# A planned spectral and gated-linear kernel: the fifth column class put together on GpSimd, with one table and one matmul per frequency

## The chip, the cores and the metric

The kernel runs on one core of one Trainium2 chip. Its time is the device time of one execution in microseconds (us); smaller is better. The engines are TensorE (PE in the profile, its weight loads PEld), VectorE (DVE), ScalarE (ACT), GpSimd (POOL) and SyncE (SP), which issues nearly all DMAs.

## What is computed

```python
xn = layernorm(x)                          # x: (1, 2048, 640) bf16
X  = rfft2(xn) * (w_r + 1j * w_i)          # 2048 x 321 complex weights
A  = irfft2(X, s=(2048, 640))
B  = ((xn @ w_gate) * (xn @ w_up)) @ w_down    # 640 -> 1536 -> 640, no nonlinearity
out = x + bf16(A) + B
```

Two branches share the normalized input: a global spectral filter over rows and columns, and a bilinear gated unit.

## The kernel before

**Stages.** The 2048 rows are held as 16 row blocks of 128 (block b, line 356 on). Each block is normalized: statistics by VectorE (`bn_stats`, L756, `bn_aggr`, L765) for blocks 0 to 5 or by ScalarE (two passes with an accumulator, L738 and L747) for the others, a square root on ScalarE (L775), a reciprocal (L782), and the scaling. For blocks 0 to 3 the scaling is two VectorE instructions, `sub` (L792, subtract the mean, which needs no root) and `mul` (L798); for the others it is one (L799). Blocks 0 to 3 are transposed by PE (`T0`, L818), the others by a DMA transpose (L806).

The gated branch is `GU` (PE, L948 for four blocks at a time, L968 for the first blocks), its evictions `eG` (ScalarE L684 or VectorE L685), the product `H` (L984, L985), and at the end the accumulations `ACC` (L1224), which share their PSUM bank with the last step of the spectral branch, `IV` (L1236), and go out through `FINA`, `FIN` and the output DMAs.

The spectral branch splits the 640 columns by residues (`S1` to `S5`, VectorE, L860 to L895) and the rows by a 64-point transform (`R`, PE, L908). Then 16 steps t of two frequencies each follow, which is the stage that the change is about: `D` (PE, L1025) transforms along columns, `eD` evicts, `C` (PE, L1045) finishes the rows, `WM` (VectorE, L1062 for four column classes, L1068 for the fifth) multiplies with the filter weights, and `IA` (PE, L1116 and L1118) starts the way back for each of the 32 frequencies q; `eIA` evicts it. After all 32 comes `I` (PE, L1147), `eI`, the recombination `V1` to `V5` on VectorE, and `IV`.

**The two ways of complex multiplication.** The 321 spectral columns fall into five classes. For classes one to four, `WM` writes the products with w_r and w_i of two steps t (a pair), `SM` (L1089, L1090) adds and subtracts halves of the partitions into the tile `L`, and `JA`, `JB` (L1101 and a copy on L684 or L685) fill the mirrored half of `L`. `IA` then needs one matmul per class, with the table `ti[:, q, 0]`. For the fifth class there is no addition: `WM` writes its two products into `Y5` (three buffers, `_NY`), `NS` on GpSimd (L1077 to L1079, three instructions for each t) makes mirrored and negated copies, and PE does the complex addition by accumulating two matmuls (L1118) with the tables `ti[:, q, 0]` and `ti[:, q, 1]`:

```python
for k in range(4):
    c.e.matmul(ps[:, bk, 64 * k:64 * k + 64], yl[:, k:512:4], v_ti[:, q, 0, :], start=True, stop=True)
for i in range(2):
    ins = c.e.matmul(ps[:, bk, 256:320], v_y5[:, yr, g, 128 * i:128 * i + 128], v_ti[:, q, i, :],
                     start=(i == 0), stop=(i == 1))
```

**What sets the order.** Every task above is created by `T(...)` in a fixed sequence, with the engines that it may run on and a duration that was assumed for it. The list `_PLAN` gives, for each task by its number in that sequence, the engine (0 PE, 1 ScalarE, 2 VectorE, 3 GpSimd, 4 SP) and the PSUM bank. `replay` (L151) follows the list; the engines run their tasks strictly in that order. `compute_waits` (L196) turns dependencies into semaphore waits; buffers that share memory depend on each other. The name of any place in the list is found by counting the tasks in order of creation.

**The head.** PE first runs 40 warm-up matmuls (L720) on a tile that VectorE sets to zero (L696), then `T0_0`, ten small matmuls (`fill`, L709), and the first `GU` groups, as their weights land. Of the down-projection weights, blocks 7 to 11 are loaded early; blocks 0 to 6 share memory with the table `ti` and are loaded when the last `IA` has read it.

Of the kernel before, what the change touches and what calls it, by code (L numbers as in the profile page):

```python
# [71 lines left out]
class _Sched(object):  # L72
# [123 lines left out]
    def compute_waits(self):  # L196
        allt = sorted(self.tasks, key=lambda t: (t.start, t.tid))
# [58 lines left out]
def _build_tables():  # L256
# [65 lines left out]
    ti = np.zeros((128, _NQ, 2, 64), np.float64)  # L322
    for q in range(_NQ):
        k = _rows(q, npm, nk1)
        ph = two_pi * ((s1[:, None] * k[None, :]) % _S) / _S
        c = np.exp(-1j * ph)
        pm = np.broadcast_to(npm[None, :], (64, 64))
        f = np.where(ck == 1, np.where(pm == 1, -1j, 1j), 1.0 + 0j)
        if q == 0:
            f = (ck == pm).astype(np.complex128)  # L330
        fm = c * f
        im = (np.conj(c) * f / _S).T
        tf[0:64, q, n_re] = fm.real
        tf[0:64, q, n_im] = fm.imag
        tf[64:128, q, n_re] = -fm.imag
        tf[64:128, q, n_im] = fm.real
        ti[n_re, q, 0] = im.real
        ti[n_im, q, 0] = -im.imag
        ti[n_re, q, 1] = im.imag
        ti[n_im, q, 1] = im.real  # L340
# [21 lines left out]
_WD_LOADS = ((7, 12), (0, 2), (2, 4), (4, 6), (6, 7))  # L362
_FT_ORDER = (7, 8, 9, 10, 11, 0, 1, 2, 3, 4, 5, 6)
# [6 lines left out]
_NY = 3  # L370
# [29 lines left out]
def _d_act(n):  # L400
# [4 lines left out]
    (12, 4, -1), (0, 1, -1), (13, 4, -1), (176, 1, -1), (175, 4, -1), (8, 2, -1), (19, 2, -1), (9, 3, -1), (177, 4, -1),  # L405
    (18, 2, -1), (20, 2, -1), (11, 0, 0), (23, 2, -1), (21, 1, -1), (22, 2, -1), (24, 2, -1), (29, 2, -1), (25, 0, 2),
    (28, 2, -1), (26, 1, -1), (27, 2, -1), (178, 4, -1), (10, 0, 4), (14, 4, -1), (30, 2, -1), (33, 2, -1), (31, 1, -1),
    (32, 2, -1), (187, 0, 5), (34, 2, -1), (185, 0, 4), (188, 1, -1), (35, 0, 6), (15, 4, -1), (37, 2, -1), (192, 0, 5),
    (190, 0, 0), (186, 1, -1), (189, 2, -1), (38, 2, -1), (179, 4, -1), (36, 1, -1), (39, 2, -1), (180, 4, -1), (181, 4, -1),
    (197, 0, 1), (40, 2, -1), (48, 2, -1), (41, 1, -1), (43, 2, -1), (42, 2, -1), (193, 1, -1), (195, 0, 2), (44, 2, -1),  # L410
    (47, 2, -1), (202, 0, 3), (200, 0, 4), (182, 4, -1), (191, 1, -1), (196, 1, -1), (198, 1, -1), (49, 2, -1), (50, 1, -1),
    (16, 4, -1), (194, 2, -1), (201, 1, -1), (45, 0, 2), (52, 2, -1), (51, 2, -1), (183, 4, -1), (53, 2, -1), (207, 0, 6),
    (46, 1, -1), (184, 4, -1), (199, 2, -1), (118, 2, -1), (54, 0, 7), (205, 0, 2), (1, 4, -1), (203, 1, -1), (204, 2, -1),
    (55, 1, -1), (210, 0, 3), (212, 0, 7), (217, 0, 5), (208, 1, -1), (17, 4, -1), (215, 0, 4), (119, 2, -1), (206, 1, -1),
    (209, 2, -1), (120, 2, -1), (56, 2, -1), (211, 1, -1), (60, 2, -1), (59, 2, -1), (2, 4, -1), (3, 4, -1), (57, 2, -1),
    (68, 1, -1), (69, 1, -1), (213, 1, -1), (220, 0, 0), (121, 2, -1), (4, 4, -1), (58, 2, -1), (70, 1, -1), (216, 1, -1),
    (61, 2, -1), (218, 1, -1), (62, 1, -1), (122, 2, -1), (63, 2, -1), (222, 0, 1), (5, 4, -1), (214, 2, -1), (64, 2, -1),
    (125, 0, 2), (221, 1, -1), (71, 1, -1), (223, 1, -1), (123, 0, 6), (126, 1, -1), (219, 2, -1), (227, 0, 4), (127, 2, -1),
    (232, 0, 5), (225, 0, 0), (72, 1, -1), (230, 0, 1), (224, 2, -1), (128, 2, -1), (6, 4, -1), (7, 4, -1), (228, 1, -1),
    (66, 2, -1), (78, 1, -1), (79, 1, -1), (237, 0, 4), (226, 1, -1), (129, 2, -1), (235, 0, 0), (73, 2, -1), (80, 1, -1),  # L420
    (233, 1, -1), (229, 2, -1), (81, 1, -1), (130, 2, -1), (231, 1, -1), (82, 1, -1), (240, 0, 5), (76, 2, -1), (131, 2, -1),
    (238, 1, -1), (134, 0, 2), (74, 2, -1), (236, 1, -1), (83, 2, -1), (234, 2, -1), (242, 0, 4), (84, 2, -1), (65, 4, -1),
    (245, 0, 1), (67, 4, -1), (241, 1, -1), (75, 4, -1), (88, 1, -1), (77, 4, -1), (239, 2, -1), (135, 1, -1), (252, 0, 0),
    (247, 0, 5), (136, 2, -1), (243, 1, -1), (89, 1, -1), (244, 2, -1), (246, 1, -1), (132, 0, 2), (137, 2, -1), (90, 1, -1),
    (91, 1, -1), (86, 2, -1), (248, 1, -1), (250, 0, 1), (249, 2, -1), (255, 0, 4), (92, 1, -1), (98, 1, -1), (251, 1, -1),
    (85, 4, -1), (87, 4, -1), (437, 4, -1), (438, 4, -1), (93, 2, -1), (99, 1, -1), (138, 2, -1), (439, 4, -1), (253, 1, -1),
    (257, 0, 5), (256, 1, -1), (100, 1, -1), (258, 1, -1), (96, 2, -1), (254, 2, -1), (101, 1, -1), (139, 2, -1), (260, 0, 1),
    (262, 0, 0), (267, 0, 4), (94, 2, -1), (263, 1, -1), (133, 1, -1), (102, 1, -1), (261, 1, -1), (259, 2, -1), (140, 2, -1),
    (265, 0, 5), (103, 2, -1), (266, 1, -1), (440, 4, -1), (268, 1, -1), (270, 0, 0), (143, 0, 2), (264, 2, -1), (441, 4, -1),
    (104, 2, -1), (272, 0, 1), (124, 1, -1), (141, 0, 4), (269, 2, -1), (442, 4, -1), (108, 1, -1), (271, 1, -1), (273, 1, -1),  # L430
    (277, 0, 6), (149, 2, -1), (274, 2, -1), (109, 1, -1), (275, 0, 7), (280, 0, 0), (443, 4, -1), (142, 1, -1), (282, 0, 1),
    (444, 4, -1), (276, 1, -1), (278, 1, -1), (147, 0, 4), (281, 1, -1), (445, 4, -1), (145, 0, 6), (150, 2, -1), (446, 4, -1),
    (285, 0, 0), (106, 2, -1), (110, 1, -1), (283, 1, -1), (447, 4, -1), (146, 1, -1), (111, 1, -1), (287, 0, 1), (279, 2, -1),
    (112, 1, -1), (144, 1, -1), (292, 0, 6), (151, 2, -1), (286, 1, -1), (290, 0, 7), (293, 1, -1), (113, 2, -1), (448, 4, -1),
    (284, 2, -1), (152, 2, -1), (288, 1, -1), (116, 2, -1), (291, 1, -1), (297, 0, 2), (474, 4, -1), (475, 4, -1), (289, 2, -1),
    (476, 4, -1), (295, 0, 3), (114, 2, -1), (153, 2, -1), (302, 0, 0), (294, 2, -1), (162, 2, -1), (298, 1, -1), (296, 1, -1),
    (95, 4, -1), (97, 4, -1), (105, 4, -1), (299, 2, -1), (303, 1, -1), (154, 0, 6), (148, 1, -1), (107, 4, -1), (300, 0, 1),
    (477, 4, -1), (301, 1, -1), (156, 0, 2), (158, 0, 4), (159, 1, -1), (305, 0, 0), (155, 1, -1), (478, 4, -1), (160, 0, 4),
    (310, 0, 1), (479, 4, -1), (163, 2, -1), (480, 4, -1), (481, 4, -1), (307, 0, 6), (308, 1, -1), (304, 2, -1), (115, 4, -1),
    (312, 0, 7), (306, 1, -1), (164, 2, -1), (315, 0, 6), (317, 0, 0), (309, 2, -1), (313, 1, -1), (157, 1, -1), (311, 1, -1),  # L440
# [82 lines left out]
def _build(nc, A_x, A_w_r, A_w_i, B_w_gate, B_w_up, B_w_down, out, opts=None):  # L523
# [3 lines left out]
    with es:  # L527
# [167 lines left out]
        def em_wz(c):  # L695
            return c.e.memset(v_dum, 0.0)  # L696
# [651 lines left out]
```

## Time and profile before

| What | Value |
|---|---|
| Median of 8 runs | 199.52 us (199.22 to 200.2) |
| The profiled execution | 199.36 us |
| Its span in the profile | 197.0 us |
| PE busy | 190.5 us, 97% of the span |
| VectorE busy | 177.6 us, 90% |
| ScalarE busy | 137.9 us, 70% |
| GpSimd busy | 28.4 us, 14%, 53 instructions |
| DMA | 23.78 MB, mean 121 GB/s |

The profile covers the span from the first to the last instruction of the program; the profiled execution's time is 2.36 us longer. Busy time of PE counts matmuls whose ends are modelled, so that a matmul row's mean is longer than the distance from one matmul to the next; the distance is read from the starts in the timeline. A few matmul records are missing (404 of the 420 on L948 are there).

### The profile page before, as it was taken

The numbers are of one execution on the slowest core, as the hardware profiler recorded it, in microseconds if no ns is written. First come the engines' busy times: TensorE is split into PE (matmuls) and PEld (weight loads), VectorE is DVE, ScalarE is ACT, GpSimd is POOL, SyncE is SP. The second block draws the span as 40 slices with busy tenths as digits, with TensorE's granted clock in tenths as the row PEclk, the third lists the DMA queues.
The fourth block names the chain that finished last, engine by engine and source line by source line (L and its number), as shares of the span: only waits on it lengthen the run. The fifth ranks groups of instructions, "written<-read, shape, count | busy, mean of one in ns | idle before, by whom it ended". The sixth has DMA issues, their size and how long they took to land.

```text
span 197.0 us, 4284 instructions
## 1 busy us (share of the span) xinstructions
PE 190.5 (97%) x1607; PEld 122.4 (62%) x1623; DVE 177.6 (90%) x396; ACT 137.9 (70%) x299; POOL 28.4 (14%) x53
## 2 busy tenths in 40 slices
PE   7799999999999999999999999999999999999995
PEld 7698645444554555555555555557777777777774
DVE  3799999999999989999899998995999999989743
ACT  3378999999965789999999999966414342334220
POOL 0000000000000003545163460760000000000000
PEclk9999999999999999999999999999999999999999
DMA  6999995245549232542452402003400434233422
GB/s 178 305 328 372 388 137 100 47 120 120 129 88 296 86 85 54 133 101 56 117 148 55 120 17 67 2 3 104 128 3 0 136 100 124 76 103 119 147 70 67
DMA packets 29667, 23.78 MB, mean 121 GB/s; under 512 B 10576, under 2 KB 27600, under 8 KB 29520
## 3 DMA queue, kind: packets, MB, share of 16 engines
q1 hardware_dynamic: 28848, 23.16, 42.6%
q10 hardware_dynamic: 800, 0.36, 0.6%
q8 instruction: 13, 0.21, 0.5%
q14 instruction: 6, 0.05, 0.1%
HBM read 18.92 MB, written 2.62 MB: 109 GB/s over the span
## 4 chain that ended last, share of the span: by engine, by line
PE 88%; DVE 6%; ACT 1%; issue 1%; DMA 1%
PE ps L948 41%; PE ps L1224 26%; PE ps L968 7%; PE ps L1147 2%; PE ps L1236 2%; PE ps L908 2%; PE ps L1116 2%; PE ps L1025 2%; PE ps L1045 2%; DVE arena L685 1%; ACT arena L684 1%; DVE arena L1062 1%; DMA arena<-in_A_x_dram 1%; PE ps L1118 1%; DVE arena L756 1%
## 5 line engine op out<-in xcount | busy, mean ns | idle before, releaser
L684 ACT ACTIVATE arena<-ps 128x512 bf16<-128x512 f32 (+6 forms) x245 | 118.4, 525 | 49.2 <-PE ps L1236 21.4
L948 PE MATMUL ps<-arena 128*128 128x512 bf16 x404 | 94.7, 379 | 1.2 <-ACT arena L684 0.3
L948 PEld LDWEIGHTS ps<-arena 128*128 128x128 bf16 x420 | 38.7, 98 | 41.5 <-ACT arena L684 1.3
L1224 PE MATMUL ps<-arena 128*128 128x320 bf16 (+2 forms) x396 | 57.2, 295 | 0.0
L1224 PEld LDWEIGHTS ps<-arena 128*128 128x128 bf16 x396 | 37.5, 98 | 13.3
L1077 POOL COPY arena<-arena 128x126 bf16<-128x126 bf16 x16 | 9.3, 581 | 104.3 <-DVE arena L1068 104.3
L1062 DVE TENSOR_TENSOR arena<-ps,arena 128x256 bf16<-128x256 f32 x64 | 22.7, 417 | 1.5 <-PE ps L1045 1.0
L984 DVE TENSOR_TENSOR arena<-arena 128x512 bf16<-128x512 bf16 x42 | 18.0, 429 | 0.7
L968 PE MATMUL ps<-arena 128*128 128x128 bf16 (+1 forms) x160 | 13.8, 246 | 1.0 <-issue 0.6
L968 PEld LDWEIGHTS ps<-arena 128*128 128x128 bf16 x160 | 12.2, 98 | 2.2 <-issue 0.7
L1079 POOL TENSOR_SCALAR arena<-arena 128x130 bf16<-128x130 bf16 x16 | 11.6, 728 | 0.0
L1263 DVE TENSOR_TENSOR arena<-arena 128x640 bf16<-128x640 bf16 x15 | 7.2, 487 | 4.2 <-ACT arena L684 4.1
L685 DVE CAST arena<-ps 128x512 bf16<-128x512 f32 (+3 forms) x15 | 8.4, 578 | 2.4 <-PE ps L1118 1.7
L1025 PEld LDWEIGHTS ps<-arena 128*128 128x128 bf16 x160 | 7.5, 98 | 3.9 <-ACT arena L684 0.7
L1116 PEld LDWEIGHTS ps<-arena 128*128 128x128 bf16 x128 | 7.8, 119 | 3.1 <-issue 0.8
L1025 PE MATMUL ps<-arena 128*128 128x64 bf16 (+1 forms) x160 | 8.7, 193 | 0.3 <-ACT arena L684 0.3
L1078 POOL COPY arena<-arena 128x126 bf16<-128x126 bf16 x16 | 8.6, 538 | 0.0
L1116 PE MATMUL ps<-arena 128*128 128x64 bf16 x128 | 8.4, 199 | 0.1
L747 ACT ACTIVATE arena<-arena 128x640 bf16<-128x640 bf16 x10 | 8.3, 832 | 0.1
L860 DVE TENSOR_TENSOR arena<-arena 128x768 f32<-128x768 bf16 (+1 forms) x10 | 8.0, 800 | 0.0
L1068 DVE TENSOR_TENSOR arena<-ps,arena 128x130 bf16<-128x130 f32 x32 | 8.0, 293 | 0.0
L1236 PE MATMUL ps<-arena 128*128 128x320 bf16 (+2 forms) x33 | 7.6, 295 | 0.0
(65 smaller groups left out, 203.0 us busy)
## 6 DMA issues: line engine op xcount, KB each, us to landing
arena<-in_A_x_dram SPq DMA_DIRECT2D x20, 160.0 KB, 2.9
arena<-in_A_w_r_dram SPq DMA_DIRECT2D x30, 80.2 KB, 2.2
arena<-in_A_w_i_dram SPq DMA_DIRECT2D x30, 80.2 KB, 2.2
out_dram<-arena SPq DMA_DIRECT2D x15, 160.0 KB, 1.8
arena<-in_B_w_gate_dram SPq DMA_DIRECT2D x4, 320.0 KB, 5.4
arena<-in_A_x_dram SPq DMA_DIRECT2D x1, 1280.0 KB, 9.9
arena<-c_tf SPq DMA_DIRECT2D x4, 256.0 KB, 10.1
arena<-c_ti SPq DMA_DIRECT2D x2, 512.0 KB, 4.9
```

What stands on the lines that cost most here:

```text
L684: return c.e.activation(dst, src, _ACTF.Copy)
L685: return c.e.tensor_copy(dst, src)
L948: ins = c.e.matmul(ps[:, bk, :], v_gw[:, w, j, ft, :], v_xt[:, j, rows], start=(j == 0), stop=(j == 4))
L968: ins = c.e.matmul(ps[:, bk, w * n:(w + 1) * n], v_gw[:, w, j, ft, :], v_xt[:, j, rows], start=(j == 0), stop=(j == 4))
L984: return c.e.tensor_tensor(v_ht[:, ft0, rows], v_gbf[:, rr, 0, :], v_gbf[:, rr, 1, :], _OP.mult)
L1025: ins = c.e.matmul(ps[:, bk, k * 64:k * 64 + n], v_uq[:, k, t, :], v_fd[:, k * 128 + w * n: k * 128 + w * n + n], start=True, stop=True)
L1062: c.e.tensor_tensor(dst, xh, wv, _OP.mult)
L1077: c.e.tensor_copy(yg[:, :, 65:128], yg[:, :, 257:320])
L1079: return c.e.tensor_scalar(yg[:, :, 128:193], yg[:, :, 256:321], -1.0, None, _OP.mult)
L1116: c.e.matmul(ps[:, bk, 64 * k:64 * k + 64], yl[:, k:512:4], v_ti[:, q, 0, :], start=True, stop=True)
L1224: ins = c.e.matmul(ps[:, bk, 0:sl3.stop - sl3.start], v_ht[:, ft, a * 128:(a + 1) * 128], v_wd[:, ft, sl3], start=(ft == _FT_ORDER[0]), st ...
L1236: return c.e.matmul(ps[:, bank_of(own), 0:sl3.stop - sl3.start], v_sm[:, 2, :], v_v[:, a, sl3], start=False, stop=True)
```

## The change

The fifth class is handled as the other four are. `WM` writes its two products of a pair of steps into one `Y5` (no longer three buffers). `NS` is gone. In its place, five tasks for each of the eight pairs: `X5A` and `X5B` copy the w_i product to the other half of the partitions (one of them negated), `S5M` adds, and `J5A` and `J5B` fill the mirrored part of a new tile `L5`. They may run on GpSimd, ScalarE or VectorE; the new list puts 30 of the 40 on GpSimd. `IA` has one matmul for the fifth class, with a contiguous 128-column weight tile, and `ti` loses its second table. With `ti` halved, only blocks 0 to 3 of the down-projection share its memory; blocks 4 to 11 load early, and the accumulation order follows.

In the head, blocks 0 to 3 are scaled by one instruction (`sub_apart` 0), block 3 takes its statistics on ScalarE (`act_set`), the warm-up and fill matmuls read a constant tile of ones and wait for no memset, there are 12 fill matmuls in place of 10, and `bn_stats` of blocks 1 to 3 no longer has to follow the `mul` of the block before. Each GpSimd task now waits for the one before it. The whole of `_PLAN` is replaced (998 entries for 981).

```diff
     def compute_waits(self):
+        for d, t in zip(self.order["pool"][:-1], self.order["pool"][1:]):
+            t.deps.add(d)
...
-        ti[n_re, q, 0] = im.real
-        ti[n_im, q, 0] = -im.imag
-        ti[n_re, q, 1] = im.imag
-        ti[n_im, q, 1] = im.real
+        ti[n_re, q] = im.real
+        ti[n_im, q] = -im.imag
...
-_WD_LOADS = ((7, 12), (0, 2), (2, 4), (4, 6), (6, 7))
-_FT_ORDER = (7, 8, 9, 10, 11, 0, 1, 2, 3, 4, 5, 6)
+_WD_LOADS = ((4, 8), (8, 12), (0, 2), (2, 4))
+_FT_ORDER = (4, 5, 6, 7, 8, 9, 10, 11, 0, 1, 2, 3)
...
-        b_y5 = alloc("Y5", _NY * 2 * 324)
+        b_y5 = alloc("Y5", 2 * 4 * 66)
+        b_l5 = alloc("L5", 2 * 4 * 128)
+        b_x5 = alloc("X5", 4 * 66)
...
+        v_one = nc.const_aps.tensor(1.0, (128, 128), _BF)
...
-        def em_wz(c):
-            return c.e.memset(v_dum, 0.0)
-        T("warm_zero", "dve", 150.0, em_wz, writes=[(b_dum, None)], prio=-1.0)
...
-        nfill = opts.get("nfill", 10)
+        nfill = opts.get("nfill", 12)
...
-        aset = set(opts.get("act_set", ())) | set(range(opts.get("act_stats", 6), 16))
+        aset = set(opts.get("act_set", (3,))) | set(range(opts.get("act_stats", 6), 16))
...
-                    if 1 <= b <= 3:
-                        bns[0].deps.add(muls[b - 1])
...
-                if b < opts.get("sub_apart", 4):
+                if b < opts.get("sub_apart", 0):
...
                 for w in range(2):
-                    ins = c.e.tensor_tensor(d5[w], ps[:, bk:bk + 2, 256:321], wt[:, w, :, 0:321:5], _OP.mult)
+                    ins = c.e.tensor_tensor(v_y5[:, w, 2 * pb:2 * pb + 2, 0:65], ps[:, bk:bk + 2, 256:321], wt[:, w, :, 0:321:5], _OP.mult)
...
-            def em_ns(c, yr=yr):
-                yg = v_y5[:, yr]
-                c.e.tensor_copy(yg[:, :, 65:128], yg[:, :, 257:320])
-                c.e.tensor_copy(yg[:, :, 193:256], yg[:, :, 1:64])
-                return c.e.tensor_scalar(yg[:, :, 128:193], yg[:, :, 256:321], -1.0, None, _OP.mult)
...
+            def em_x5a(c):
+                dst, src = v_x5[0:64, :, 0:65], v_y5[64:128, 1, :, 0:65]
...
+                return c.e.tensor_scalar(dst, src, -1.0, None, _OP.mult)
+            def em_x5b(c):
+                return copy_on(c, v_x5[64:128, :, 0:65], v_y5[0:64, 1, :, 0:65])
...
+            def em_s5(c, lr=lr):
+                return c.e.tensor_tensor(v_l5[:, lr, :, 0:65], v_y5[:, 0, :, 0:65], v_x5[:, :, 0:65], _OP.add)
...
+            def em_j5a(c, lr=lr):
+                return copy_on(c, v_l5[0:64, lr, :, 65:128], v_l5[64:128, lr, :, 1:64])
+            def em_j5b(c, lr=lr):
+                dst, src = v_l5[64:128, lr, :, 65:128], v_l5[0:64, lr, :, 1:64]
...
+                return c.e.tensor_scalar(dst, src, -1.0, None, _OP.mult)
...
-                    for k in range(4):
-                        c.e.matmul(ps[:, bk, 64 * k:64 * k + 64], yl[:, k:512:4], v_ti[:, q, 0, :], start=True, stop=True)
-                    for i in range(2):
-                        ins = c.e.matmul(ps[:, bk, 256:320], v_y5[:, yr, g, 128 * i:128 * i + 128], v_ti[:, q, i, :],
-                                         start=(i == 0), stop=(i == 1))
+                    for k in range(5):
+                        st = yl[:, k:512:4] if k < 4 else v_l5[:, lr, q % 4, :]
+                        ins = c.e.matmul(ps[:, bk, 64 * k:64 * k + 64], st, v_ti[:, q, :], start=True, stop=True)
```

Counted off by name, the new list differs so from the old one, in tasks:

| Task | ScalarE before, after | VectorE before, after | GpSimd before, after |
|---|---|---|---|
| `eG` | 95, 93 | 5, 7 | |
| `eD` (two instructions each) | 30, 28 | 2, 4 | |
| `eIA` | 27, 29 | 5, 3 | |
| `eI` and `eR` | 29, 29 | 3, 3 | |
| `JA` and `JB` | 3, 5 | 13, 11 | |
| `X5A` and `X5B` | 0, 6 | 0, 1 | 0, 9 |
| `S5M` | | 0, 2 | 0, 6 |
| `J5A` and `J5B` | 0, 0 | 0, 1 | 0, 15 |
| `NS` (three instructions each) | | | 16, 0 |
| Statistics of block 3 | 0, 2 | 3, 0 | |
| `sub` | | 4, 0 | |

PE has 350 tasks in both. SP has 143 before and 142 after, one load of down-projection weights fewer.

## The prediction

> **What bounds the kernel now.** I read first the page's engine totals and its chain of work, to see which engine sets the end.
>
> ```profile
> PE 190.5 (97%) x1607; PEld 122.4 (62%) x1623; DVE 177.6 (90%) x396; ACT 137.9 (70%) x299; POOL 28.4 (14%) x53
> ...
> PE 88%; DVE 6%; ACT 1%; issue 1%; DMA 1%
> ```
>
> PE is busy for 97% of the span and makes up 88% of the chain, so time is saved by taking work from PE or by closing its gaps. Then the busy times by stretch, over the stage of 16 spectral steps (columns: stretch, length, PE, PEld, DVE, ACT and POOL busy, clock, DMA share, GB/s):
>
> ```profile
> 70.00:80.00 10.00, 9.95 (x90) 5.56 (x90) 9.45 (x24) 9.02 (x20) 3.15 (x6) 1.00 0.33 86
> 80.00:90.00 10.00, 9.61 (x112) 5.82 (x112) 9.44 (x28) 9.83 (x23) 4.63 (x10) 1.00 0.46 115
> 90.00:100.00 10.00, 9.83 (x81) 5.30 (x80) 9.43 (x27) 9.43 (x22) 2.67 (x4) 1.00 0.32 84
> 100.00:110.00 10.00, 9.89 (x99) 5.55 (x99) 9.21 (x24) 9.73 (x24) 6.15 (x11) 1.00 0.34 88
> 110.00:120.00 10.00, 9.95 (x86) 5.48 (x86) 9.04 (x25) 9.66 (x22) 4.48 (x8) 1.00 0.32 78
> 120.00:131.00 11.00, 10.54 (x98) 5.83 (x99) 10.50 (x32) 9.72 (x22) 4.81 (x10) 1.00 0.05 18
> ```
>
> Three engines are nearly full here at once. Of 61 us PE works 59.77, ScalarE 57.39 and VectorE 57.07; PE stands for 1.23 us. Only GpSimd has room (25.89). Between 14 and 70 us PE loses 0.38 us, and from 131 us to the tail next to nothing.
>
> Third, PE's timeline at the first two `IA`, for the distance between starts:
>
> ```profile
> 81.27 0.30 PE L1116 MATMUL ps<-arena 128*128 128x64 bf16 x4
> 81.41 0.22 PE L1118 MATMUL ps<-arena 128*128 128x64 bf16 x2
> 81.47 0.30 PE L1116 MATMUL ps<-arena 128*128 128x64 bf16 x4
> 81.60 0.22 PE L1118 MATMUL ps<-arena 128*128 128x64 bf16 x2
> 82.11 0.32 PE L1025 MATMUL ps<-arena 128*128 128x64 bf16 x5 [0.28 <-ACT arena L684]
> ```
>
> Four matmuls of L1116 take 0.14 us of PE, the two of L1118 take 0.06, that is 0.03 each; the printed 0.22 is latency. The last line is a stall of the kind that this stage has: PE waits for a ScalarE eviction.
>
> Fourth, GpSimd's timeline, two `NS` in succession:
>
> ```profile
> 76.18 0.29 POOL L1077 COPY arena<-arena 128x126 bf16<-128x126 bf16 x1 [75.37 <-DVE arena L1068]
> 76.41 0.29 POOL L1078 COPY arena<-arena 128x126 bf16<-128x126 bf16 x1
> 76.74 0.55 POOL L1079 TENSOR_SCALAR arena<-arena 128x130 bf16<-128x130 bf16 x1
> 77.92 0.81 POOL L1077 COPY arena<-arena 128x126 bf16<-128x126 bf16 x1 [0.63 <-DVE arena L1068]
> 78.67 0.76 POOL L1078 COPY arena<-arena 128x126 bf16<-128x126 bf16 x1
> 79.40 0.94 POOL L1079 TENSOR_SCALAR arena<-arena 128x130 bf16<-128x130 bf16 x1
> ```
>
> The same three instructions take 1.13 us in the first group and 2.51 in the second. Beside the first VectorE runs `WM` (one operand in PSUM), beside the second `SM` (L1089, L1090, two operands in SBUF).
>
> **What the Trainium skill says.** "SBUF — State Buffer", section "Who interferes with whom": a VectorE instruction with two SBUF inputs contends with a GpSimd instruction that reads SBUF, and the later one blocks. The 0.29 against 0.81 us agree. "GPSIMD Engine Reference", section 3.1: an addition of two tensors costs some 2.2 ns an element (4497 ns for 2048); no row here shows one. Its section 2.1 says that consecutive Pool instructions are no barrier between the cores of GpSimd, so that a reader of another core's output needs a semaphore wait; the added chain of waits is that. "TensorE: Matmul & The Clock Gate", section "Wait — 56ns, not 53.3ns?": starts of small matmuls come no closer than about 25 ns. The 30 ns here are nearly at that floor, so the one matmul removed is worth its 30 ns and no more.
>
> **The change, part by part.**
>
> *IA.* One of six matmuls goes in each of 32: 32 x 0.03 = 0.96 us less of PE. It lies on PE's path in a stage where PE has 1.23 us of gaps, so it counts in full if the gaps stay. Ends: 0 (another engine sets the pace) and 0.96.
>
> *The fifth class.* Off GpSimd go 48 instructions, mean 581 + 538 + 728 = 1847 ns for each t, 3.7 us a pair. In come five a pair, of 252 to 260 elements. A copy: from 0.29 (all fixed cost) to 0.60 (all per element); I take 0.5. A negating copy: 0.55 to 1.1; I take 0.95. The addition: the page's 0.57 up to 1.1; I take 0.8. No row shows GpSimd reading one half of the partitions and writing the other; I take it as free and keep the upper end in the range. A chain wholly on GpSimd is 2 x 0.5 + 2 x 0.95 + 0.8 = 3.7 us alone and, slowed as NS is on average (1.85 against 1.13), 6.1. That is 4.2 us more between `WM` and `IA` than the 1.85 before. The new list covers it: between `C_1` and the first `IA` stood five `GU` of 5 x 0.216 = 1.08 us, now ten, 5.4 us more. At the last pair the cover is thinner: between `C_14` and `IA_30` stand five `GU` and five `IA`, 6.2 us, against `WM` 1.7, `H` 0.4, `SM` 1.4, two copies 0.9 and `J5B` 0.3 on VectorE, 4.7 us.
>
> *A new wait.* `Y5` has one buffer where there were three. `WM` of the next pair waits for `X5A`, `X5B` and `S5M`; behind it VectorE's whole queue waits, and behind that `IA` and the `H` products. On VectorE 3.2 to 4.2 us of other tasks stand between the pairs in the list; X5A + X5B + S5M are 2.25 us alone, 3.7 slowed. The tightest place is `S5M_9`, on VectorE itself, behind `eIA_10`, `SM_9` and `JB_7` (2.3 us), waiting for two GpSimd copies (1.45 alone, 2.4 slowed). I take 0.1 us of stall there.
>
> *Work moved between engines, same stage.* ScalarE: one `eG` less in the stage (-0.60), two `eD` less (-4 x 0.434 = -1.74), two `eIA` more (+0.88), two `JA`/`JB` more (+2.10), six `X5` at some 0.4 (between zero and the 0.434 of 64x321; +2.4): +3.0, so 60.4. VectorE: two `eD` more (4 x 0.494 = +1.98), two `JA`/`JB` less (-0.85), two `eIA` less (-0.98), four small fifth-class tasks at 0.3 (+1.2): +1.4, so 58.4. The stage has 61 - 0.96 = 60.0 us. Busy times overlap at their ends by some per cent, so ScalarE just fits, with no slack. The old stage lost 1.23 us with slack; I put 0.3 us more of PE gaps (ends -1.0, all gaps planned away, and +1.5, ScalarE's and VectorE's surplus paid in full).
>
> *The head.* Four `sub` (4 x 382 ns) go, `mul` takes 450 in place of 386 ns, `bn_stats` and `bn_aggr` of block 3 leave VectorE. What it buys shows here:
>
> ```profile
> 4.85 0.39 DVE L798 TENSOR_SCALAR arena<-arena 128x640 bf16<-128x640 bf16 x1
> 6.50 1.28 PE L968 MATMUL ps<-arena 128*128 128x128 bf16 x20 [0.38 <-DVE arena L765]
> 8.65 3.51 PE L968 MATMUL ps<-arena 128*128 128x128 bf16 x60 [0.60 <-issue]
> 12.00 0.44 PE L818 MATMUL ps<-arena 128*128 128x128 bf16 x5
> ```
>
> In the list half of block 1's statistics (0.44) now stands ahead of `rs_0`, whose root is ready at 4.62: `mul_0` ends near 5.43 rather than 5.24, `T0_0` starts near 5.6. ScalarE runs `sd_1` before the first eviction, so that the first `GU` starts near 6.95 instead of 6.50. But `T0_1` no longer waits for a late `mul_1` (about 7.15 instead of 7.35), and behind it stand `GU_0_0` and `GU_0_1`, whose weights are there, where PE stood until 8.65 for weights issued at 2.68 and landed 5.9 us later. From 6.95, eight groups of ten matmuls (0.56 each) and `T0_1` (0.28), with 0.1 of waiting, end near 11.8 instead of 12.0: 0.2 us gained (ends -0.1, 0.5). The memset that goes let PE wait 0.2 us, but what follows the warm-up waits for `mul_0`: 0. Two more fill matmuls lie in that wait: 0.
>
> *Down-projection weights and ti.* One DMA less, a smaller table, eight blocks early instead of five. Nothing waits for these loads in the waits of before; 0. *Chained GpSimd waits*: GpSimd ran in order anyway; 0.
>
> **Sum**, against the profiled execution: 199.36 - 0.96 - 0.2 + 0.3 = 198.5. The median of the runs lies 0.16 above it: 198.7 us.
>
> **Rivals.**
>
> 1. *The matmul was hidden.* ScalarE, at 60.4 us in a 60.0 us stage, becomes the bound and PE's saving turns into waits such as the 0.28 above. Against it: ScalarE's busy times overlap. Then only head gain is left, less some waiting: about 199.5.
>
> 2. *GpSimd on VectorE's path (slower).* If X5A + X5B + S5M exceed the 3.5 us or so that stand between pairs on VectorE, every pair adds the excess. At 4.0 us, 8 x 0.5 = 4.0; less the 1.6 us that VectorE has free in the stage, +2.4: 198.7 + 2.4 = about 201. It decides from a mean of 1.33 us each; my slowed estimate is 1.24. For it: 0.29 became 0.81 beside `SM`, and `SM` follows `WM` at once. Against it: in most pairs ScalarE or VectorE takes one of the three.
>
> 3. *A better order.* The new list closes most gaps of the stage: 198.7 - 1.0 = 197.7.
>
> **How the numbers follow.** This kernel's runs can tell about 0.2%, 0.4 us, from no change: faster is below 199.1, slower above 199.9. Chances: forecast 0.55 (own range 198.1 to 199.1), rival 1 0.19, rival 2 0.19, rival 3 0.07. Faster: 0.55 + 0.07, less 0.02 at the forecast's upper edge, 0.60; same 0.20, slower 0.20. The range leaves out half of rival 3 and two thirds of rival 2: 197.9 to 200.6.
>
> **What would show it.** `IA` near 0.17 us from start to start, not 0.20. `T0_2` near 11.8. PE's idle time in the stage 1 to 2 us: below 0.5 is rival 3; waits of PE for L684 growing by 1 us, rival 1; VectorE waiting at L1062 or at the addition for POOL, rival 2. GpSimd copies above 1.3 us on average would make the prediction wrong, as would a stall at the first `I`, where no `ACC` is left in front of the last `IA`.

## The result and the profile after

| What | Before | After |
|---|---|---|
| Median | 199.63 us (32 runs, 199.22 to 200.45) | 200.56 us (11 runs, 200.42 to 201.54) |
| Ratio | | 1.0048 (95% interval 1.0036 to 1.0059) |
| The profiled execution, its span | 199.36, 197.0 us | 200.58, 198.8 us |

The change makes the kernel slower by 0.9 us, where 0.8 us faster was forecast. The engine totals and the chain of work of the changed kernel:

```profile
PE 191.7 (96%) x1577; PEld 122.2 (61%) x1593; DVE 180.7 (91%) x394; ACT 142.2 (72%) x307; POOL 23.1 (12%) x35
...
PE 60%; DVE 18%; ACT 13%; issue 3%; DMA 3%; SPq 1%
```

PE was 88% of the chain and is now 60%; VectorE went from 6 to 18% and ScalarE from 1 to 13%. So the end is no longer set by PE alone. The same stretches of the spectral stage as before:

```profile
70.00:80.00 10.00, 9.85 (x92) 5.22 (x91) 9.64 (x24) 9.05 (x20) 1.97 (x3) 1.00 0.33 85
80.00:90.00 10.00, 9.22 (x65) 4.79 (x67) 9.79 (x25) 9.72 (x19) 4.61 (x6) 1.00 0.46 112
90.00:100.00 10.00, 9.06 (x97) 5.35 (x98) 9.79 (x27) 9.37 (x22) 3.63 (x5) 1.00 0.29 72
100.00:110.00 10.00, 9.50 (x79) 5.15 (x79) 9.80 (x26) 9.38 (x20) 4.96 (x6) 1.00 0.32 82
110.00:120.00 10.00, 9.89 (x94) 5.40 (x93) 9.73 (x25) 9.72 (x24) 4.41 (x6) 1.00 0.20 52
120.00:131.00 11.00, 10.79 (x88) 5.49 (x89) 10.73 (x33) 10.75 (x23) 2.09 (x4) 1.00 0.12 32
```

The third busy column is VectorE: 9.73 to 9.80 in the four middle rows, where it was 9.04 to 9.44. It is full. In the second and third rows PE is down to 9.22 and 9.06 where it was 9.61 and 9.83. From the first `D` to the first `I` the stage lasts 64.7 us instead of 64.1, although 9 `ACC` matmuls of 0.136 us, 1.2 us of work, no longer stand in it but after it.

What VectorE does longer is seen in its groups of instructions in the stage. First the two halves of `SM` before, then after (busy us, mean ns of one):

```profile
L1089 DVE TENSOR_TENSOR arena<-arena 64x1024 bf16<-64x1024 bf16 x8 | 5.5, 688 | 0.3
L1090 DVE TENSOR_TENSOR arena<-arena 64x1024 bf16<-64x1024 bf16 x8 | 5.5, 687 | 0.1
```

```profile
L1075 DVE TENSOR_TENSOR arena<-arena 64x1024 bf16<-64x1024 bf16 x8 | 6.5, 809 | 0.1
L1074 DVE TENSOR_TENSOR arena<-arena 64x1024 bf16<-64x1024 bf16 x8 | 6.2, 778 | 0.3
```

The instructions are the same; their means grew by 0.09 and 0.12 us. `H` grew from 432 to 474 ns, while `WM`, with one operand in PSUM, stayed at 417. One pair in the timeline of the changed kernel shows why, VectorE first, GpSimd second:

```profile
77.65 0.42 DVE L981 TENSOR_TENSOR arena<-arena 128x512 bf16<-128x512 bf16 x1
78.10 0.77 DVE L1074 TENSOR_TENSOR arena<-arena 64x1024 bf16<-64x1024 bf16 x1
78.89 1.07 DVE L1075 TENSOR_TENSOR arena<-arena 64x1024 bf16<-64x1024 bf16 x1
```

```profile
77.80 0.53 POOL L689 COPY arena<-arena 64x260 bf16<-64x260 bf16 x1 [76.97 <-DVE arena L1061]
78.50 0.92 POOL L1105 TENSOR_TENSOR arena<-arena 128x260 bf16<-128x260 bf16 x1 [0.17 <-ACT arena L1095]
```

The first half of `SM` starts while a GpSimd copy runs and takes 0.77 instead of 0.69; the second starts while the addition `S5M` runs and takes 1.07. The rows of `SM`, `H`, `JA` and `JB` that start while GpSimd works are sorted under "The addition alone in halves" below. `JA` and `JB` read one operand only and grew too: the VectorE copies (L689, 64x1024) from 423 to 494 ns, the negating ones (L1086) from 422 to 541.

Most of PE's waits in the stage of the changed kernel stand ahead of `C` (L1041; L688 and L689 are evictions):

```profile
PEld ps L1041 <- issue: 2.8, 5, 0.8
PEld ps L1041 <- ACT arena L688: 2.1, 5, 0.6
...
PE ps L1041 <- ACT arena L688: 1.2, 2, 0.8
...
PE ps L1041 <- DVE arena L689: 0.5, 1, 0.5
...
PE ps L1041 <- POOL arena L1105: 0.2, 1, 0.2
```

By the distances between starts PE stands for some 3.2 us ahead of `C`, and nowhere ahead of `C` in the old kernel. The kernel says how VectorE's delay gets there: `hold(tc, wm)` (L1066) makes `C` wait for everything that its `WM` would wait for, at the start of a pair `SM` and `S5M` of the pair before. `SM` of that pair and then `C`, twice:

```profile
78.89 1.07 DVE L1075 TENSOR_TENSOR arena<-arena 64x1024 bf16<-64x1024 bf16 x1
80.06 0.43 PE L1041 MATMUL ps<-arena 128*128 128x321 bf16 x2
...
95.33 0.79 DVE L1075 TENSOR_TENSOR arena<-arena 64x1024 bf16<-64x1024 bf16 x1
96.37 0.43 PE L1041 MATMUL ps<-arena 128*128 128x321 bf16 x2 [0.75 <-ACT arena L688]
```

`C` starts 0.10 and 0.26 us after `SM` ends, and the one at 104.01 again 0.26 after; in the kernel whose `IA` doesn't wait (below) the three distances are the same. These three make 1.8 of the 3.2 us. The profile puts two of them down to ScalarE, but the evictions that these two `C` wait for had ended earlier.

### The profile page after: what moved, and what is told of

The parts are those of the page before. It is cut to its first block, busy times and chain, and to the rows that moved or that the text cites. A ratio compares the mean times of both kernels' runs of the same rounds, so it can differ in the third digit from the quotient of the medians.

```text
span 198.8 us, 4223 instructions
## 1 busy us (share of the span) xinstructions
PE 191.7 (96%) x1577; PEld 122.2 (61%) x1593; DVE 180.7 (91%) x394; ACT 142.2 (72%) x307; POOL 23.1 (12%) x35
## 4 chain that ended last, share of the span: by engine, by line
PE 60%; DVE 18%; ACT 13%; issue 3%; DMA 3%; SPq 1%
PE ps L1237 26%; PE ps L945 23%; ACT arena L688 12%; DMA arena<-in_A_x_dram 3%; PE ps L1160 2%; PE ps L1249 2%; DVE arena L1058 2%; DVE arena L981 2%; PE ps L905 2%; SPq L682 1%; PE ps L1132 1%; DVE arena L858 1%; PE ps L1021 1%; DVE arena L857 1%; DVE arena L796 1%
## 5 line engine op out<-in xcount | busy, mean ns | idle before, releaser
L688 ACT ACTIVATE arena<-ps 128x512 bf16<-128x512 f32 (+7 forms) x241 | 116.0, 531 | 46.2 <-PE ps L1249 24.6
L981 DVE TENSOR_TENSOR arena<-arena 128x512 bf16<-128x512 bf16 x42 | 18.7, 447 | 0.4
L689 POOL COPY arena<-arena 64x252 bf16<-64x252 bf16 (+1 forms) x13 | 6.3, 486 | 92.4 <-DVE arena L1061 91.1
L689 DVE CAST arena<-ps 64x321 bf16<-64x321 f32 (+4 forms) x20 | 10.7, 550 | 0.9 <-PE ps L945 0.4
L746 ACT ACTIVATE arena<-arena 128x640 bf16<-128x640 bf16 x11 | 9.3, 842 | 0.1
L1041 PE MATMUL ps<-arena 128*128 128x321 bf16 x32 | 7.0, 300 | 2.1 <-ACT arena L688 1.2
L737 ACT ACTIVATE arena<-arena 128x640 bf16<-128x640 bf16 x11 | 8.3, 752 | 0.6 <-DMA arena<-in_A_x_dram 0.5
```

What stands on the lines that cost most here:

```text
L688: return c.e.activation(dst, src, _ACTF.Copy)
L689: return c.e.tensor_copy(dst, src)
L746: return c.e.activation(v_jk, v_x[:, b, :], _ACTF.Square, scale=-1.0, bias=v_m32[:, b:b + 1], accum_out=v_ss[:, b:b + 1])
L981: return c.e.tensor_tensor(v_ht[:, ft0, rows], v_gbf[:, rr, 0, :], v_gbf[:, rr, 1, :], _OP.mult)
```

## The theories

- A, contention: GpSimd's instructions that read SBUF keep VectorE's two-operand instructions waiting; VectorE, already nearly full, becomes the bound.
- B, the chain: `IA` waits for the end of the chain of five tasks, or the next pair's `WM` for its middle (the prediction's second rival).
- C, the list: the new order is worse in itself.
- D, the ten fifth-class tasks on ScalarE and VectorE, and what else moved there, overfill these engines.

## The experiments

Each was timed beside the kernel before, whose medians were 199.51 to 199.67 us, so ratios with their intervals are compared. Differences in us are differences of ratios times 199.6.

### Parts of the change alone

**One matmul, old list** (L1117 of before; half of the fifth class's sum is left out).

```diff
-                    for i in range(2):
+                    for i in range(1):
```

> The kernel before with the second of the two fifth-class matmuls (L1118) left out in each IA, so that a part of the result is missing; everything else, list and GpSimd work included, is as before. It prices the removed matmul alone. If PE sets the pace of the spectral stage, as the prediction's sum has it: 32 x 0.03 = 0.96 us less, ratio 0.995 against the kernel before. If ScalarE or VectorE sets the pace: ratio 1.000.

Measured: 199.27 us, ratio 0.9985 (0.9971 to 0.9999). Taking 0.96 us of PE out of the stage gains 0.3 (by the interval 0.0 to 0.6). Most of PE's saving is lost to waiting. That ScalarE and VectorE set much of the stage's pace already before the change is the likely reason; which wait took it isn't shown.

**The head alone.** The head's edits on the old kernel, with the new list until well before the stage, then the old list.

> The kernel before with the head of the changed one alone (no memset, ones for the warm-up, 12 fill matmuls, one scaling instruction for blocks 0 to 3, block 3 by ScalarE, and the changed list up to the last GU of block pair 2); fifth class, ti and the rest of the list as before. The prediction's step: 0.2 us gained, 199.4, ratio 0.999. A rival: the later first GU is not made up for, or order changes spill over, 199.8, ratio 1.001 or more.

Measured: 200.60 us, 1.0051 (1.0039 to 1.0064). Inconclusive: at the seam PE stands 1.46 us for an eviction, which neither full list does:

```profile
23.28 1.02 PE L940 MATMUL ps<-arena 128*128 128x512 bf16 x4 [1.46 <-ACT arena L683]
```

Hence a second try with the seam at the first `D`, and a third with the one matmul besides.

> The old kernel with the new head and the new list up to the first product of the fifth class's stage (rows 0-3 scaled in one instruction, twelve fillers on the ready-made constant, the fourth row's statistics on ScalarE), and the old fifth class and old list from there. If the head is a gain of its own, as the prediction took it (0.2 us) and as the first D product 0.1 us earlier in the changed kernel suggests, 199.3 to 199.5, with the first D at 71.2 to 71.4. If the head is worth nothing, or costs, because the first row lands and is scaled later, 199.6 to 200.0 with the first D at 71.4 to 71.8. More than that would again be a seam between two lists that were not made for each other.

Measured: 199.51 us, 0.9990 (0.9982 to 0.9998), 0.2 us gained (by the interval 0.0 to 0.4). The trace doesn't show where: the profiled execution had its first `D` only at 71.54, after the old kernel's 71.41.

> The old kernel with the new head and list up to the first D product, and from there the old list with the old fifth class of which the second matmul of each frequency is left out (the output lacks that half of the class's sum). Alone the two were worth 0.2 and 0.3 us against the old kernel. If they add up, 199.0 to 199.3. If the stage's end is set by ScalarE and VectorE, so that a head that is earlier by 0.1 and a lighter TensorE gain the same time only once, 199.3 to 199.5.

Measured: 199.08 us, 0.9974 (0.9965 to 0.9982), 0.5 us. The two parts add up, 0.2 + 0.3, as closely as these intervals can tell.

### The fifth class made light

Three kernels with the changed kernel's list, in which `IA` reads other data for the fifth class and the tasks named are two columns wide (in the first all forty, in the second the thirty on GpSimd, in the third the other ten). One of the five tasks in the second:

```diff
-                return copy_on(c, v_x5[64:128, :, 0:65], v_y5[0:64, 1, :, 0:65])
+                n = 2 if c.e is nc.gpsimd else 65
+                return copy_on(c, v_x5[64:128, :, 0:n], v_y5[0:64, 1, :, 0:n])
```

> The changed kernel with all forty X5, S5M and J5 tasks cut to two columns of each frequency, and IA reading a part of L as its fifth weights; list, engines, waits and buffers stay, most of the fifth class is left out. Theory A (work and contention: the fifth-class tasks on ScalarE and VectorE, and GpSimd's chains slowing VectorE's two-operand instructions, fill both engines and PE waits): 198.2 to 198.8, ratio 0.993 to 0.996, below the kernel before. Theory B (the five-link chain delays IA and the next WM): the same, since the chain is short too. Theory C (the new list itself is worse, with evictions on VectorE and IA late): near 200.3, ratio 1.003 or more.

> The changed kernel with the thirty GpSimd tasks of the fifth class cut to two columns, the ten on ScalarE and VectorE whole; IA reads a part of L as its fifth weights (the fifth class is mostly left out). Theory A, if contention is the larger share: VectorE gets back the 2 to 2.5 us by which SM, H and copies are longer, 198.6 to 199.3, ratio 0.995 to 0.998. Theory A, if the ten tasks are the larger share: about 200.2, ratio 1.003. Theory C: about 200.4.

> The changed kernel with the ten fifth-class tasks on ScalarE and VectorE cut to two columns, the thirty on GpSimd whole; IA reads a part of L as its fifth weights (the fifth class is partly left out). ScalarE loses about 1.2 us of work, VectorE about 0.6. Theory A, contention the larger share: 200.0 to 200.4, ratio 1.002 to 1.004. Theory A, the ten tasks the larger share: 199.4, ratio 0.999. Theory B: no change, 200.5, ratio 1.0045.

| Light tasks | Time | Ratio |
|---|---|---|
| none (the changed kernel) | 200.56 us | 1.0048 (1.0036 to 1.0059) |
| all forty | 198.48 us | 0.9935 (0.9910 to 0.9961) |
| thirty on GpSimd | 199.65 us | 1.0007 (0.9989 to 1.0025) |
| ten on ScalarE and VectorE | 200.11 us | 1.0035 (1.0021 to 1.0049) |

C falls as the cause: with the same list and a light fifth class the kernel is 1.3 us faster than before. The fifth class costs 2.3 us (1.0048 - 0.9935). The GpSimd part alone costs 0.8, and with it `SM` is back at its old length:

```profile
L1074 DVE TENSOR_TENSOR arena<-arena 64x1024 bf16<-64x1024 bf16 x8 | 5.5, 688 | 0.4 <-PE ps L1137 0.2
L1075 DVE TENSOR_TENSOR arena<-arena 64x1024 bf16<-64x1024 bf16 x8 | 5.5, 687 | 0.1
```

The ten others cost 0.3 with GpSimd at work and 1.4 without: the shares depend on what else is full and don't add up to a fixed sum. A and D both hold so far.

**`IA` without the wait for the chain** (it reads data that is there).

```diff
-                       reads=[(b_l, ("r", 3 * lr, 3 * lr + 3)), (b_l5, ("r", 3 * lr, 3 * lr + 3)),
+                       reads=[(b_l, ("r", 3 * lr, 3 * lr + 3)),
```

> The changed kernel with IA reading a part of L as its fifth weights and no longer waiting for J5A and J5B (the fifth class does not reach the result); all forty tasks still run in full, and WM still waits for Y5. It takes the end of the chain off PE's path and leaves all work and contention. Theory A: as the changed kernel, 200.3 to 200.6, ratio 1.004 to 1.005. Theory B: 199.6 or below, ratio 1.000 or less.

Measured: 200.66 us, 1.0053 (1.0040 to 1.0066), the changed kernel's time. That half of B falls.

**GpSimd writing only**: its thirty tasks as memsets of the same tiles, in two or four pieces.

```diff
+                if c.e is nc.gpsimd:
+                    for g_ in range(4):
+                        ins = c.e.memset(v_l5[:, lr, 1 * g_:1 * g_ + 1, 0:65], 0.0)
+                    return ins
```

> The changed kernel with the thirty GpSimd tasks replaced by memsets of the same tiles, cut in two or four pieces so that they last about as long but read nothing from SBUF (the fifth class is left out; IA reads a part of L in its place); ten tasks on ScalarE and VectorE as they are, all waits as they are. It keeps the chain's length and takes away GpSimd's reads beside VectorE's two-operand instructions. Theory A, contention: as with short GpSimd tasks, 199.4 to 199.8, ratio about 1.000, with SM back at 0.70 us. Theory B: as the changed kernel, 200.4, ratio 1.004.

Measured: 199.57 us, 0.9994 (0.9981 to 1.0007), and `SM` at its old length. This is in line with reading as what disturbs VectorE, but doesn't show it. A task of memsets lasted only some 0.4 us, no memset had more than 0.18 us left when a half of `SM` started, and one VectorE copy (`JA` or `JB`) that had 0.23 us of a memset ahead of it was 0.09 us longer.

### Where the lengthening comes from

**All forty on GpSimd**, whole (the list with another engine number for ten tasks).

> The changed kernel with all forty fifth-class tasks on GpSimd, at their places in the list; the result is whole. ScalarE loses six instructions (2.3 us), VectorE four (1.1 us), GpSimd gains ten. Theory A, ScalarE and VectorE work as the bound: 199.6 to 200.0, ratio 1.000 to 1.002. Theory A, contention as the larger share: no better, about 200.5, since GpSimd reads more. Theory B, the chain's length: 201 or more, ratio over 1.007.

Measured: 202.13 us, 1.0125 (1.0111 to 1.0139), 1.5 us slower than the changed kernel, although ScalarE and VectorE have less to do. Not an answer by itself: VectorE's instructions are longer, and `C` also waits for the addition (1.8 us), which is the other half of B.

**The order**, two tests: `SM` directly behind its `WM`s in the new list, and an `H` ahead of `SM` in the old one (in seven of eight pairs). VectorE's order in the first pair, new list, then old:

```diff
- WM_0 WM_1 H_29 SM_1 eD_4_0
+ WM_0 WM_1 SM_1 H_29 eD_4_0
...
- WM_0 WM_1 SM_1 H_29 JB_1
+ WM_0 WM_1 H_29 SM_1 JB_1
```

> The changed kernel with one order altered: on VectorE each SM (the two 64x1024 subtractions and additions of a pair) stands directly behind the second WM of its pair, as in the old list; the H, eviction or small tasks that stood between come after it. Nothing else is changed. If what lengthens SM is that GpSimd's copies of the same pair are already running when SM comes (whoever starts first keeps the other waiting), SM falls from 0.79 and 0.84 us to 0.70 to 0.75, VectorE has some 1 us less to do in the stage, and the time is 199.5 to 200.1. If GpSimd's reads lengthen VectorE's instructions whatever the order, or H and the evictions moved behind SM keep TensorE waiting instead, 200.4 to 200.9.

Measured: 205.69 us, 1.0290 (1.0268 to 1.0311). Far beyond both expectations. The first half of `SM` is back at 0.69 us, but `H` now comes second: six of them start while the addition runs and take 0.71 to 0.91 us. And the tasks pushed back were needed: PE waits 5.7 us for `H` (L981), before it can reuse its banks (the waits of its weight loads, in the second line, lie in the same gaps). In the stretch with the longest of these waits the granted clock was 0.83.

```profile
PE ps L945 <- DVE arena L981: 5.7, 5, 2.4
...
PEld ps L945 <- DVE arena L981: 4.3, 3, 2.3
```

> The old kernel with one order altered, the reverse test: on VectorE, in seven of the eight pairs, the next H stands between the last WM and SM, as the new list has it, so that GpSimd's four-part sums of the old fifth class can start ahead of SM. If who starts first decides, SM grows from 0.70 to 0.75 to 0.95 us, and the time from 199.5 to 199.8 to 200.4. If the order is nothing, or VectorE has slack enough in the old list, SM stays at 0.70 to 0.72 and the time at 199.4 to 199.7.

Measured: 201.39 us, 1.0083 (1.0062 to 1.0103); but `SM` did not grow (688 and 685 ns). VectorE waits 3.9 us for ScalarE's evictions ahead of the earlier `H`. `SM` here starts after GpSimd's old copies in four of eight pairs and isn't lengthened. This doesn't refute A: in all four the copy had only 0.12 us left. Two `H` that started with 0.28 and 0.29 us of such a copy left took 0.55 and 0.56 us instead of 0.42. Why that is so the table below shows; an instruction of 252 or 260 elements can have more left than one of 126 or 130.

**Halves**: each GpSimd task of the fifth class as two instructions of half the width. Work, order and engines stay.

```diff
+                if c.e is nc.gpsimd:
+                    for g_ in (slice(0, 2), slice(2, 4)):
+                        ins = c.e.tensor_tensor(v_l5[:, lr, g_, 0:65], v_y5[:, 0, g_, 0:65], v_x5[:, g_, 0:65], _OP.add)
+                    return ins
```

> The changed kernel with each of the 30 fifth-class tasks on GpSimd cut into two instructions of half the width (two frequencies each), so that one GpSimd instruction keeps VectorE waiting for half as long. If the length of a GpSimd instruction sets how long an SM or H is kept waiting, SM falls to 0.72 to 0.78 us and the time to 199.9 to 200.3. If what counts is the sum of what GpSimd reads and writes beside VectorE, SM stays at 0.79 and 0.84 and the 30 more GpSimd starts make it 200.6 to 201.2.

Measured: 199.44 us, 0.9993 (0.9979 to 1.0007): 1.1 us less than the changed kernel, with GpSimd busy for 30.5 instead of 22.8 us of the stage. VectorE's busy time in the stage falls from 62.9 to 60.3 us. (The profiled execution began the stage late and took 200.55; only its stage is read here.) The longer chain has its price: `C` waits 1.0 us for the addition in this trace, in three places.

```profile
L1075 DVE TENSOR_TENSOR arena<-arena 64x1024 bf16<-64x1024 bf16 x8 | 5.8, 722 | 0.1
L1074 DVE TENSOR_TENSOR arena<-arena 64x1024 bf16<-64x1024 bf16 x8 | 5.5, 687 | 0.3
```

**The addition alone in halves.**

> The changed kernel with only the addition S5M cut in halves where GpSimd has it (six of eight pairs); copies and negating copies stay whole. In the changed kernel's trace an SM or H that meets a running S5M lasts 0.39 us longer, seven or eight times in the stage, and one that meets a copy or negating copy of 252 or 260 elements 0.09 longer. If that is the whole account, this edit wins most of what halving everything won (1.1 us): 199.5 to 200.0. If copies and negating copies cost as much in sum, it wins a third or less: 200.1 to 200.5.

Measured: 199.77 us, 1.0021 (1.0008 to 1.0035): 0.5 us of the 1.1. The rows of `SM`, `H`, `JA` and `JB` in the traces of before, after and the two kernels with halves, sorted by what GpSimd was running as they started, how much of it was left, and how much longer the row was than one beside an idle GpSimd (0.69 us for `SM`, 0.42 for the others):

| Running on GpSimd | Left of it (us) | VectorE's row longer by (us) |
|---|---|---|
| copy of 126 or 130 elements (before, halves) | 0.11 to 0.15 | 0.00 |
| the same | 0.21 to 0.23 (two rows) | 0.07 to 0.08 |
| copy of 252 or 260 (after) | 0.22 to 0.24 | 0.08 to 0.09 |
| the same | 0.32 (one `H`) | 0.18 |
| addition of 130 (halves) | 0.26 to 0.29 | 0.12 to 0.14 |
| the same | 0.43 (one copy) | 0.28 |
| addition of 260 (after) | 0.51 to 0.57 | 0.37 to 0.42 |
| negating copy of 126 or 130 (before, halves), beside `SM` or `H` | 0.28 to 0.40 | 0.00 |
| the same, beside `H` | 0.47 to 0.51 | 0.08 to 0.12 |
| the same, beside `JA` or `JB` | 0.57 | 0.00 |
| negating copy of 252 or 260 (after), beside `SM` | 0.69 to 0.71 | 0.09 to 0.11 |

For copies and additions of every size the two columns differ by 0.14 us: in all traces of this case together by 0.137 to 0.151 in the 103 rows with 0.21 to 0.63 us left. So VectorE's instruction, coming second, waits until 0.14 us before the recorded end of GpSimd's, and what counts there is how much is left, and not the width or the number of inputs as such. Behind a negating copy it mostly goes on earlier, some 0.4 to 0.6 us before the recorded end for 126 or 130 elements and 0.6 to 0.7 for 252 or 260. Where GpSimd came second in these four traces, VectorE's rows kept their length to within 0.02 us. Summed over these rows of one trace:

| Kernel | VectorE's rows longer by, in sum (us) | Ratio |
|---|---|---|
| before | 0.3 | 1 |
| after | 3.8 (2.4 of it behind additions) | 1.0048 |
| addition in halves | 2.6 | 1.0021 |
| all thirty in halves | 1.3 | 0.9993 |

### Other places for the work

**All forty on GpSimd, in halves.**

> The changed kernel with all forty fifth-class tasks on GpSimd, each cut into two instructions of half the width. It differs from the run with all forty whole on GpSimd (202.1) only in the halves, and from the run with thirty halved (199.4) only in where ten tasks run. If what made all forty on GpSimd slow was the whole-width instructions that VectorE waits for, and the ten tasks cost ScalarE and VectorE 0.5 us or more where they are, 198.6 to 199.3. If the chain of five tasks on one slow engine comes too late for IA, or keeps the next pair's products back, 199.8 to 201.

Measured: 206.57 us, 1.0384 (1.0354 to 1.0413). VectorE is hardly lengthened (0.7 us in sum), but the chain is now too long: the addition (L1115) is late, the next `WM` may not overwrite `Y5` before it, and `hold` puts that wait on `C`.

```profile
PEld ps L1041 <- issue: 8.5, 7, 2.3
PE ps L1041 <- POOL arena L1115: 6.8, 7, 1.8
DVE arena L1058 <- PE ps L1041: 6.5, 8, 1.3
```

This is the prediction's second rival, in a kernel that isn't the changed one. Moving the ten tasks to GpSimd costs more than they cost where they are, whole (202.13) or in halves; so D can't be had back that way.

**Quarters.** What ran has the negating copy `X5A` on GpSimd in quarters and the additions still in halves; the expectation was written for quarters of the addition, another kernel.

> The changed kernel with the fifth-class tasks on GpSimd in halves, and the addition S5M in four quarters (65 elements each). An SM or H that meets a running S5M lasted 0.39 us longer with the whole addition and 0.14 with halves; with quarters it should be 0 to 0.05. VectorE then has 0.7 us less to wait for in the stage than with halves, and the time is 199.0 to 199.4. If the stage no longer hangs on VectorE, or the addition, now some 2 us for a pair with four starts, holds back the next pair (whose last products overwrite what it reads), 199.4 to 200.5.

Measured: 201.46 us, 1.0099 (1.0084 to 1.0113), 2.1 us more than with halves, with `C` waiting 3.5 us for the addition. The likely reason is the chain again, with four starts in `X5A`. Quarters of the addition weren't tried.

**The addition on VectorE**, directly behind `SM`; then the same with GpSimd's copies in halves. VectorE's order in the first pair:

```diff
- WM_0 WM_1 H_29 SM_1 eD_4_0
+ WM_0 WM_1 H_29 SM_1 S5M_1 eD_4_0
```

> The changed kernel with all eight additions S5M on VectorE, directly behind SM of their pair (two of eight were there); copies and negating copies where they were, whole. VectorE gets 6 additions of 0.30 us = 1.8, and loses the 0.39 us of each SM, H or copy that met a running S5M, 2.3 us in the trace of the changed kernel: 0.5 us less. The chain of the pair is shorter by 0.6 us as well. By that account 199.9 to 200.3. If the addition waits on VectorE for a negating copy that is not done, with everything behind it, 200.6 to 202.

> As the run with all additions on VectorE behind SM, and the copies and negating copies that stay on GpSimd in halves. Of the 1.5 us by which whole copies lengthened VectorE's instructions most goes, so 0.5 to 1.0 less than that run: 199.2 to 199.7 if it meets no wait; with a wait of the addition for its copies, the 200.6 to 202 of that run, or more, since halves make the copies last longer in sum.

Measured: 199.82 us, 1.0011 (1.0002 to 1.0020), and 199.46 us, 0.9992 (0.9981 to 1.0002), the first a little below what was expected, the second within it. VectorE is busy for 61.9 and 60.7 us of the stage, six more additions of 0.30 us among it, against 62.9 in the changed kernel: doing these additions costs it 1.8 us, and the same additions on GpSimd made its rows 2.4 us longer. The sum of the table above is 1.5 us in the first of the two and 0.3 in the second.

No version with the whole computation and the new fifth class beats the old kernel by more than can be told; the new head on the old kernel is 0.1% below it.

## Why the prediction was wrong

**The step that failed** is "Work moved between engines, same stage": "VectorE: two `eD` more ... +1.4, so 58.4", and from it "I put 0.3 us more of PE gaps". From the first `D` to the first `I` VectorE was busy 59.1 us before and 62.9 after, +3.8. With GpSimd's tasks light the same list gives 59.4, so 3.5 us is time that GpSimd adds to VectorE's own instructions; the rows themselves say 3.8. The prediction put this at nothing. I had quoted the section of the Trainium skill ("SBUF — State Buffer", "Who interferes with whom") that says the later of the two blocks, and the trace of before showed it with GpSimd as the later one (0.29 against 0.81). I used it only that way, as slower GpSimd, and asked of VectorE only whether it waits for GpSimd's results. But the new chain starts on GpSimd as soon as `WM` ends, with one longer instruction after another, and the new list has an `H` or another task between `WM` and `SM` in all eight pairs, so that `SM`, `H`, `JA` and `JB` often come second.

The old trace gave little warning, but some. `SM` has one length there, 0.69 us, even where it starts behind a GpSimd copy, since those copies had at most 0.14 us left. Two `H`, though, came second by more and were 0.08 and 0.12 us longer than the rest. One of them, GpSimd first:

```profile
89.91 0.54 POOL L1079 TENSOR_SCALAR arena<-arena 128x130 bf16<-128x130 bf16 x1
89.94 0.54 DVE L984 TENSOR_TENSOR arena<-arena 128x512 bf16<-128x512 bf16 x1
```

A second step failed beside it: "it counts in full if the gaps stay". Of the 0.96 us of `IA` the old list gives back only 0.3.

**Term by term.**

- *Head*, -0.2: the time agrees, 0.2 (0.9990, within 0.0 to 0.4). Its working is borne out by half: `T0_2` came at 11.91 instead of 12.00, forecast 11.8, and the first `D` of the changed kernel 0.11 us earlier.
- *IA*, -0.96: the size of the saving was right, 0.17 us from the start of an `IA` to the start of what follows (next rows), its effect was not. In the old list it gains 0.3. The gaps don't stay, as in the first rival; that it is ScalarE that takes them is not shown.

```profile
89.20 0.33 PE L1132 MATMUL ps<-arena 128*128 128x64 bf16 x5
89.37 1.03 PE L945 MATMUL ps<-arena 128*128 128x512 bf16 x4
```

- *ScalarE*, +3.0: right. 59.3 to 62.2 us in the stage.
- *Mid-stage gaps*, +0.3: the failed step. Cutting GpSimd's long instructions in halves won 1.1 us back, so some 1.1 us came from them.
- *GpSimd*: copies 0.46 and 0.53 us against 0.5, negating copies 1.01 and 1.02 against 0.95, the addition 0.89 against 0.8, all with the waits for VectorE in them; moving between the halves of the partitions showed no extra cost (shortest copy of 126 elements 0.28 us across, 0.29 within). All in their bounds.
- *The new wait* of `WM` for GpSimd, 0.1: it was sought in the wrong place. `hold` puts it on `C`, so that it can't show as a wait of VectorE at L1062 (VectorE's list has 0.4 us in the whole stage, all on PE). On PE the profile has 0.2 us of it, once.

The sum with the two terms mended: -0.2 - 0.3 + 0.3 + 1.1 = +0.9, as measured. It isn't a proof of each term, and that it comes out so exactly is in part luck: the +0.3 left for gaps has no run of its own, the intervals of the others are 0.3 us wide and more, and the light kernels show that shares depend on what else is full.

**The rivals.** The second came nearest in number (201), but not by its mechanism: of the wait for `X5A`, `X5B` and `S5M` the changed kernel has 0.2 us, and it showed as a bound only when the chain was made longer. What the stage lost isn't fully divided between the lengthening (A) and the ten tasks with the other work moved to ScalarE (D): A is shown by halves, which leave work, order and engines as they are, and by the lengths of VectorE's rows; D only by leaving work out.

## What to carry to other kernels

When work goes to an idle GpSimd beside a nearly full VectorE, count it twice: what GpSimd needs, and what VectorE's instructions lose when they start behind it (here those with two SBUF operands, and SBUF copies too); look at which comes second, and at how much of the GpSimd instruction is then left. If it must be there, cut it into shorter instructions, as long as its chain has the time, or leave the two-input operation on VectorE. And a saving on the busiest engine in a stage where three engines are above 90% can be worth a fraction of its size, here a third.

## What was not expected of the hardware

- VectorE waits for nearly all that is left of a GpSimd copy or addition, all but 0.14 us, whatever its size. That agrees with the Trainium skill's section ("SBUF — State Buffer", "Who interferes with whom"), which says that the later one blocks until the other has finished. Behind negating copies it waited for less by their spans: one with 0.69 us left made a half of `SM` 0.09 us longer. The skill ("Perfetto Trace Analysis", "GPSIMD Engine Instruction") calls GpSimd's spans unreliable, so that what is left may itself be misread; the lengths of `SM` are VectorE's.
- About half of a short GpSimd copy is a fixed cost: the shortest took 0.39 us with 252 elements, 0.28 with 126 and 0.19 with 8 (the light tasks). So halves are dear on GpSimd, whose busy time in the stage grew by a third, and yet the kernel became faster.
- `WM`, with one operand in PSUM, was never lengthened, whatever GpSimd ran: 0.40 to 0.43 us in every row of before, after and both kernels with halves.
